# From attention to experts: the order of work at the border of two phases in a fused attention and mixture-of-experts kernel

## The chip, the cores and the metric

The kernel runs on one core of a Trainium2 chip. A core has a matrix engine (TensorE, PE in the profile, with its weight loads shown as PEld), a vector engine (VectorE, DVE), an engine for activations and copies (ScalarE, ACT), a general engine (GpSimd, POOL) and a queue engine that issues transfers (SyncE, SP). Each runs its own instructions in the order in which the program lists them and waits for the others through semaphores. The metric is the device time of one execution, in microseconds (us).

## The reference

Sliding-window attention with four sink tokens over 4 batches, 8 heads, 768 positions and 64 columns per head; its output, 3072 tokens of 512 columns, goes through a two-level mixture of experts.

```
scores = scale * q @ k.T, kept where key < 4 or 0 <= query - key < 128
a = exp(scores - max); a = a / (sum(a) + 1e-9); x = a @ v      # 3072 tokens x 512
g_idx = argmax(x @ w_group)             # 4 groups
e_idx = argmax(xg @ w_expert[g])        # 4 experts in each
h = relu(xg @ w1[g, e])                 # 512 -> 1024
out[token] = g_w * e_w * (h @ w2[g, e]) # 1024 -> 512
```

## The kernel before, in words

**Attention.** Tokens are taken in 24 tiles of 128 (NI = 24). One loop over i from 0 to NI+1 works on three tiles at once: tile i gets its scores, maxima (DVE) and exponentials (ACT); tile a = i-1 gets its probabilities transposed (`trans`, on PE, into the two-bank tile `tp`), copied out of PSUM (`evac`, ACT, into `pa`), masked by two selects for each half (POOL, `pu` and `pa`) and multiplied with the values (`values`, `sink_values`), the result copied to `xT` (`out_evac`, ACT); tile b = i-2 gets its routing logits (`logits`), is transposed back (`natural`, into the same `tp`), scaled by the reciprocal of its sums (`norm`, into `xt`) and written to the DRAM tile `xd` by SP. There is one `tp` only, so `sink_t` and `natural` can write it when both `evac` have read it. In the last two rounds, i = NI and NI+1, no new scores are left ("tail"): the score banks are given back and become a ring of four banks `ph` for the experts, and the experts' work begins between the attention's instructions.

**Routing.** Tiles form four batches of six. `route` is a generator of small DVE steps for a batch (argmax, counts, positions, gate weights `cw`, a table `tab` of token numbers), with two steps on PE. Batch 1's end names the fullest expert (rank 0), and its first 256 tokens are gathered during attention (`xg`, indirect transfers by POOL). Batch 2's end gives rank 0's third tile, the late tile; batch 3's end gives rank 1's gather indices and the order of all other experts ("eid", "x2" to "x15"). `routing(k, kinds)` advances these generators by k steps; `rb` is the list of batches that are not finished. The gate weights are written into `xd` by SP (`put_gates`), in front of the gathers that read them.

**Experts.** Each weight chunk (128 x 1024 float32, 512 KB) is loaded by SP (`prefetch`, into `rw`), rounded to float32r by ACT (`whi`) and its rest is subtracted by DVE (`wlo`). During attention a chunk is rounded in two halves, a half per round (`wjob`, the second half waiting in `half`); in the tail it goes whole, and a finished chunk then also calls `prefetch`. Tokens are split the same way: `xpose` transposes a gathered tile on PE, ACT copies the rounded part to `un`, DVE the rest. A product is made of three: rounded by rounded, rounded by rest, rest by rounded. `layer1_wide` goes over eight column chunks of 128, each with 12 matmuls; `split_h` makes ReLU and its split on ACT and DVE, DVE's part one chunk later. `layer1_narrow` handles a tile of up to 128 tokens with the tokens stationary, in two halves u of 512 columns. `PARTS[0]` holds rank 0's first 256 tokens and its late tile. `early_work` is the generator for the first of these: two transposes, then eight chunks, and the late tile's transpose behind chunk number LATE, counted from 0.

**Order.** All engines take their instructions in the order written by the program. In the tail that order is written by hand in the loop below; afterwards `spend(us)` advances a planned clock `clk` by the PE time of each piece and inserts routing steps and weight jobs as long as the planned DVE time `dve` is not more than DVELAG = 1.5 ahead. A routing step costs at least the pace of the moment.

Of the kernel before, what the change touches and what calls it, by code (L numbers as in the profile page):

```python
# [14 lines left out]
AF = mybir.ActivationFunctionType  # L15
ALU = mybir.AluOpType
# [5 lines left out]
P = 128  # L22
B, H, S, D = 4, 8, 768, 64
NT = S // P
NI = B * NT
# [3 lines left out]
NDC = DM // P  # L29
G, EG, F = 4, 4, 1024  # L30
NE = G * EG
# [21 lines left out]
RAW, RAWB = 5, 4  # L53
PACE = 1.8
RPACE = 0.8
DVELAG = 1.5
XLEAD = 9
PEGAP = 1.6
REND, TSTEP = 6, 16
UNITS = {7: 3, 9: 4, 10: 9, 13: 3, 16: 10, 17: 5, 19: 4, 20: 5, 21: 4, 22: 5, NI - 1: 6}  # L60
HC = 3
LATE = 5
RUN = 1
PELAG = 2.0
DMALAG = 2.2
# [4 lines left out]
PARTS = [[dict(r=0, j0=0, T=EC * P, last=False), dict(r=0, j0=EC, T=CAPT[0] - EC * P, last=True)]]  # L70
# [64 lines left out]
def moe_attention(tc, kqT, vN, vS, nsw, wgx, w1, w2, out):  # L135
    nc = Pinned(tc)
    v = nc.vector
    with ExitStack() as top, ExitStack() as att:
# [34 lines left out]
        vts, svs, env, bat = {}, {}, {}, {}  # L173
# [618 lines left out]
        def evac(i, g):  # L792
            e = env[i]
            pa = wk.tile([P, 4, P], F32, name="pa", bufs=2)
            nc.scalar.copy(pa.rearrange("p h (f q) -> p f h q", f=2),
                           env["tp"][:, :, 4 * g * D:4 * (g + 1) * D].rearrange("p f (h q) -> p f h q", q=D))
            e["pT", g] = pT = [pa]
            if i % NT:
                for dst, sg in ((pu[g], -1), (pa, 1)):
                    nc.gpsimd.affine_select(out=dst[0:D], in_=pa[0:D], pattern=[[0, 8], [sg, D]], compare_op=ALU.is_ge,  # L800
                                            fill=0.0, base=(sg - 1) // 2, channel_multiplier=-sg)
                pT.append(pu[g])
# [51 lines left out]

        def norm(i):
            xt = wk.tile([P, DM], F32, name="xt", bufs=2)
            v.tensor_tensor(xt.rearrange("p (c j d) -> p j c d", c=NDC, j=2),
                            env["tp"][:, :, 0:NDC * D].rearrange("p j (c d) -> p j c d", c=NDC),
                            env[i]["rc"].rearrange("p (c j) -> p j c", j=2)[..., None].to_broadcast([P, 2, NDC, D]), ALU.mult)
            nc.sync.dma_start(xd[i * P:(i + 1) * P, 0:DM], xt)  # L860

        bounds = [sum(BATCHES[:k]) for k in range(len(BATCHES) + 1)]
# [19 lines left out]
                pick = {SNAP: 0, SNAPB: 1, len(BATCHES) - 1: 2}.get(k)  # L882
                rb.append([[(id(lt), x) for x in range(nb)], route(bounds[k], nb, lt, pick), None])

        def routing(k, kinds=(None, "pe", "rd")):
            while k > 0:
                if not rb or not have.issuperset(rb[0][0]):
                    return False
                kind = rb[0][2] if isinstance(rb[0][2], str) else None
                if kind not in kinds or (kind == "pe" and state["clk"] < state["at"]):  # L890
                    return False
                rb[0][2] = r = next(rb[0][1], "end")
                k -= r if isinstance(r, int) else 1
                if tail:
                    dve(0.6 if kind == "rd" else 0.25)
                state["at"] = max(state["clk"] + state["gap"], state["dve"] + 0.4)
                if rb[0][2] == "end":
                    rb.pop(0)
            return True
# [6 lines left out]
        def spend(us):  # L906
            state["credit"] += us
            state["clk"] += us
            state["route"] = min(state["route"] + us, 4.0)
            pace = RPACE if "x2" in ready else 0.1  # L910
            while state["route"] > pace and state["dve"] < state["clk"] + DVELAG and routing(1):
                state["route"] -= pace
            if state["credit"] >= PACE and (state["done"] < XLEAD or "x1" in ready) and state["dve"] < state["clk"] + DVELAG and wjob():
                state["credit"] = min(state["credit"] - PACE, 2 * PACE)
# [33 lines left out]
        def weights(*k):  # L948
            while k not in wt:
                if not wjob(True):  # L950
                    raise RuntimeError("weights out of order")
            return wt[k]

        def layer1_wide(q):
            T, o, r = q["T"], q["o"], q["r"]
            comb = T < 240
            lag = []
            if q["m"] < T:
                q["hq"] = yp.tile([P, NFC, 32], F32, name="hq", bufs=2)
            for f in range(NFC):  # L960
                ph = ps_h.tile([P, 512], F32, name="ph")
                fs = slice(f * P, (f + 1) * P)
                for c in range(NDC):
                    hi, lo = weights(1, r, c)
                    st, sp = c == 0, c == NDC - 1
                    if comb:
                        if sp:
                            nc.tensor.matmul(ph[:, 0:T], lo[:, fs], xx[:, c, o:o + T], start=False, stop=False)
                        nc.tensor.matmul(ph[:, 0:2 * T], hi[:, fs], xx[:, c, o:o + 2 * T], start=st, stop=sp)
                        if not sp:  # L970
                            nc.tensor.matmul(ph[:, 0:T], lo[:, fs], xx[:, c, o:o + T], start=False, stop=False)
                    else:
                        nc.tensor.matmul(ph[:, 0:T], hi[:, fs], xx[:, c, o:o + T], start=st, stop=False)
                        nc.tensor.matmul(ph[:, 0:T], hi[:, fs], xx[:, c, o + T:o + 2 * T], start=False, stop=False)
                        nc.tensor.matmul(ph[:, 0:T], lo[:, fs], xx[:, c, o:o + T], start=False, stop=sp)
                src = ph[:, 0:T]
                if comb:
                    src = yp.tile([P, 224], F32, name="hc", bufs=HC)[:, 0:T]
                    nc.scalar.copy(src, ph[:, T:2 * T])
                    v.tensor_tensor(src, ph[:, 0:T], src, ALU.add)  # L980
                lag.append(split_h(q, f, src))
                if len(lag) > 1:
                    drain(lag[0])
                    lag.pop(0)
                next(lag[-1]) if not comb else None
                us = T / 200 + (0.24 if comb else 0.18)
                pop_todo()
                state["freed"] += 4 if q["last"] and f == NFC - 1 else 0
                yield us
            drain(lag[0])  # L990
# [32 lines left out]
        def layer1_narrow(q):  # L1023
            T, o, r = q["T"], q["o"], q["r"]
            q["hs"] = h = yp.tile([P, F], F32, name="hs", bufs=1)
            for u in range(2):
                ph = ps_h.tile([P, 512], F32, name="ph")
                us = slice(u * 512, (u + 1) * 512)
                for c in range(NDC):
                    hi, lo = weights(1, r, c)  # L1030
                    xh, xl = xx[:, c, o:o + T], xx[:, c, o + T:o + 2 * T]
                    st, sp = c == 0, c == NDC - 1
                    nc.tensor.matmul(ph[0:T], xh, hi[:, us], start=st, stop=False)
                    nc.tensor.matmul(ph[0:T], xl, hi[:, us], start=False, stop=False)
                    nc.tensor.matmul(ph[0:T], xh, lo[:, us], start=False, stop=sp)
                    state["freed"] += u if q["last"] else 0
                    yield 0.7
                nc.scalar.copy(h[0:T, us], ph[0:T])

        def hidden_t(q, u):  # L1040
# [127 lines left out]
        for i in range(NI + 2):  # L1168
# [4 lines left out]
            if i == NI:  # L1173
                state.update(gap=0.0, dve=state["clk"])
                sps.close()
                put_gates(MAXB)
                while later:
                    gather(*later.pop(0))
                ps_h = fl.enter_context(tc.tile_pool(name="ps_h", bufs=4, space=PSUM, side="right", reuse_waits="tile"))
                tail.append(ps_h)  # L1180
                next(ew)
                next(ew)
                if half:
                    half.pop()()()
            if live:
                load_v(i)
            if i == 1:
# [4 lines left out]
            if mid:  # L1192
                trans(a)
                evac(a, 0)
                evac(a, 1)
            if live and i != 1:
                scores(i, 0)
            if later and not gates:
# [37 lines left out]
                norm_logits(b)  # L1236
            if late:
                late()
            if mid:
                values(a, 0)  # L1240
                values(a, 1)
                sink_values(a)
                out_evac(a)
            put_gates(2 if live else MAXB)
            routing(UNITS.get(i, REND) if live else TSTEP, (None, "rd"))
            if live and i % 2:
                sums(i)
            if i >= CHOOK and (i % 2 or i > NI - 4):
                prefetch(min(RAW, len(raws) + (1 if live else RAW)))
            if not live:  # L1250
                wjob()
                next(ew, None)
        att.close()
        state.update(gap=PEGAP)
        ps_t = fl.enter_context(tc.tile_pool(name="ps_t", bufs=2, space=PSUM, side="left", reuse_waits="tile"))
# [293 lines left out]
```

## Time and profile before

| what | us |
|---|---|
| median of three runs | 495.21 |
| lowest and highest run | 494.78, 497.12 |
| the profiled execution's own time | 498.14 |
| its span, first to last instruction | 496.4 |
| PE busy in it | 478.7 |
| DVE, ACT, POOL busy in it | 376.1, 327.9, 168.1 |

A profile line gives the start, the duration, the engine, the operation, the tile written and the tiles read with their shapes, and, in brackets, how long the engine had been idle before and who released it. Every operation has the same line number here, because a helper records them all; tiles are told apart by their names. In stretches of time, the busy times stand in the order PE, PEld, DVE, ACT, POOL.

### The profile page before, as it was taken

How to read it: one execution, taken by the hardware profiler on the slowest of the kernel's cores; microseconds unless marked ns; L12 is line 12 of the kernel's file. 1: busy time of each engine (PE TensorE's matmuls, PEld its weight loads, DVE VectorE, ACT ScalarE, POOL GpSimd, SP SyncE). 2: the span in 40 equal slices, each digit the busy share in tenths (PEclk: the TensorE clock that was granted, in tenths of full speed). 3: DMA queues.
4: the chain of work that ended last, by engine and by line, in shares of the span. 5: the costliest groups of instructions: out<-in, count | busy, mean ns of one | idle time of the engine just before them, and what ended most of it. 6: DMA issues, size and time to landing. Idle time of an engine off the chain costs nothing. (4 is left out here: it accounts for less than half of the span.)

```text
span 496.4 us, 14618 instructions
## 1 busy us (share of the span) xinstructions
PE 478.7 (96%) x5399; PEld 403.7 (81%) x5399; DVE 376.1 (76%) x1175; ACT 327.9 (66%) x861; POOL 168.1 (34%) x276
## 2 busy tenths in 40 slices
PE   7998999999999999999999999999999999999992
PEld 6787788887888888988989789669876979798782
DVE  7475897899989889997814875487588997889831
ACT  4887888889895335676615765377446786868731
POOL 3564454563563012512313123212232453230311
PEclk9999999999999999999999999999999999999997
DMA  7877776877986458863952338697859996996200
GB/s 201 258 221 218 234 224 219 258 234 251 300 285 204 151 162 301 274 230 109 388 230 81 108 111 302 212 353 260 311 182 366 411 325 227 383 305 207 98 22 29
DMA packets 59216, 114.71 MB, mean 231 GB/s; under 512 B 9486, under 2 KB 21774, under 8 KB 59136
## 3 DMA queue, kind: packets, MB, share of 16 engines
q1 hardware_dynamic: 54256, 100.14, 59.8%
q0 software_dynamic: 4352, 13.26, 7.8%
q8 instruction: 44, 0.72, 0.6%
q10 hardware_dynamic: 528, 0.29, 0.3%
q14 instruction: 36, 0.29, 0.2%
HBM read 100.89 MB, written 13.24 MB: 230 GB/s over the span
## 5 line engine op out<-in xcount | busy, mean ns | idle before, releaser
L105 DVE TENSOR_TENSOR wlo<-rw,whi 128x1024 fp32r<-128x1024 f32 x112 | 134.0, 1219 | 23.0 <-ACT whi L105 21.8
L105 PE MATMUL ph<-un,whi 128*128 128x256 f32 (+4 forms) x576 | 130.8, 315 | 0.0
L105 PE MATMUL po<-whi,un 128*128 128x512 f32 (+2 forms) x384 | 126.9, 396 | 0.0
L105 POOL DMA_INDIRECT out<-ot,sidx x33 | 52.9, 1603 | 213.5 <-DVE ot L105 69.8
L105 ACT CAST whi<-rw 128x1024 fp32r<-128x1024 f32 (+1 forms) x116 | 115.6, 1021 | 8.3 <-PE po L105 4.7
L105 PE MATMUL ph<-un,wlo 128*128 128x160 f32 (+4 forms) x416 | 100.4, 266 | 0.0
L105 PEld LDWEIGHTS ph<-un,whi 128*128 128x128 f32 x576 | 94.1, 189 | 1.4
L105 PEld LDWEIGHTS po<-whi,un 128*128 128x128 f32 (+1 forms) x384 | 70.8, 186 | 25.1 <-issue 6.7
L105 ACT ACTIVATE pt<-sm,st 128x136 f32<-128x136 f32 x192 | 76.0, 399 | 18.8 <-DVE st L105 18.7
L105 PE MATMUL po<-wlo,un 128*128 128x512 f32 (+3 forms) x200 | 77.8, 390 | 0.0
L105 PEld LDWEIGHTS ph<-un,wlo 128*128 128x128 f32 x416 | 77.1, 189 | 0.8
L105 POOL DMA_INDIRECT xg<-xd,gidx x33 | 37.3, 1130 | 35.5 <-DVE idz L105 25.0
L105 DVE CUSTOM_DVE_ANT_0 sm<-ps,msk 128x136 f32<-128x136 f32 x192 | 45.6, 295 | 4.2 <-PE ps L105 1.4
L105 DVE TENSOR_TENSOR hc<-ph,hc 128x160 f32<-128x160 f32 (+2 forms) x64 | 22.0, 347 | 28.0 <-ACT hc L105 26.5
L105 PEld LDWEIGHTS po<-wlo,un 128*128 128x128 f32 (+2 forms) x200 | 36.3, 182 | 7.5
L105 PE MATMUL ps<-kb,qb 64*64 64x208 f32 (+1 forms) x768 | 38.9, 339 | 2.0 <-DMA qb<-in_kqT 1.9
L105 ACT ACTIVATE ot<-po,cg 128x512 f32<-128x512 f32 (+3 forms) x25 | 17.0, 680 | 30.1 <-PE po L105 30.0
L105 ACT ACTIVATION_READ_ACCUMULATOR pt<-sm,st 128x1 f32 x192 | 36.3, 189 | 0.0
L105 ACT COPY hc<-ph 128x160 f32<-128x160 f32 (+2 forms) x64 | 19.9, 311 | 23.8 <-PE ph L105 19.1
L105 ACT ACTIVATE un<-ph 128x256 fp32r<-128x256 f32 x40 | 15.4, 385 | 28.7 <-PE ph L105 25.3
L105 PEld LDWEIGHTS ps<-kb,qb 64*64 64x64 f32 x768 | 27.1, 136 | 7.2 <-issue 2.8
L105 POOL TENSOR_SCALAR_AFFINE_SELECT pu<-pa 64x512 f32<-64x512 f32 x40 | 27.6, 691 | 14.1 <-ACT pa L105 13.9
(199 smaller groups left out, 746.3 us busy)
## 6 DMA issues: line engine op xcount, KB each, us to landing
rw<-in_w SPq DMA_DIRECT2D x128, 512.0 KB
vv<-in_vN SPq DMA_DIRECT2D x24, 512.0 KB
kb<-in_kqT SPq DMA_DIRECT2D x23, 288.0 KB
qb<-in_kqT SPq DMA_DIRECT2D x24, 256.0 KB
xd<-xt SPq DMA_DIRECT2D x24, 256.0 KB
svr<-in_vS SPq DMA_DIRECT2D x4, 192.0 KB
xg<-xd,gidx POOLq DMA_INDIRECT x33
out<-ot,sidx POOLq DMA_INDIRECT x33
```

Of the source, the lines that this page charges most:

```text
L105: r = f(*a, **k)
```

## The change

It has seven parts. (1) In round NI the transposes and copies of the last tile's probabilities come before the two token transposes of the experts instead of behind them. (2) The last half of a weight that is open in round NI-1 is rounded and split in that round and not at the start of the next. (3) In chunk 0 of rank 0's first layer, and in the first half of its late tile, the products with the rest of the tokens come last, behind all others. (4) The late tile is transposed behind chunk 6 and not 5. (5) In the tail `norm` uses eight activations on ScalarE, one for each head, in place of one multiplication on VectorE; this concerns tiles 22 and 23. (6) Routing in round NI+1 stops when one batch is left, and the paces of later steps change: 0.8 from "eid" on instead of from "x2" on, 3.0 from "x15" on. (7) At the end of both tail rounds the next chunk of layer 1 is listed ahead of the weight job.

```
+REST = 3.0
-LATE = 5
+LATE = 6
 def norm(i):
+    if tail:
+        for h in range(H):
+            nc.scalar.activation(xt[:, h * D:(h + 1) * D], env["tp"][:, h % 2, h // 2 * D:(h // 2 + 1) * D],
+                                 AF.Copy, scale=env[i]["rc"][:, h:h + 1])
+    else:
         v.tensor_tensor(xt..., env["tp"]..., env[i]["rc"]..., ALU.mult)
...
-def routing(k, kinds=(None, "pe", "rd")):
+def routing(k, kinds=(None, "pe", "rd"), till=0):
     while k > 0:
+        if len(rb) == till:
+            return False
...
-    pace = RPACE if "x2" in ready else 0.1
+    pace = REST if f"x{NE - 1}" in ready else RPACE if "eid" in ready else 0.1
...
 # layer1_wide, for each of the four row chunks c
+    elif q is PARTS[0][0] and f == 0:
+        nc.tensor.matmul(ph[:, 0:T], hi[:, fs], xx[:, c, o:o + T], start=st, stop=False)
+        nc.tensor.matmul(ph[:, 0:T], lo[:, fs], xx[:, c, o:o + T], start=False, stop=False)
+        for k in range(NDC if sp else 0):
+            nc.tensor.matmul(ph[:, 0:T], weights(1, r, k)[0][:, fs], xx[:, k, o + T:o + 2 * T],
+                             start=False, stop=k == NDC - 1)
...
 # layer1_narrow, late tile, first half
+    held_back = q is PARTS[0][1] and u == 0
     for c in range(NDC):
...
-        nc.tensor.matmul(ph[0:T], xl, hi[:, us], start=False, stop=False)
+        if not held_back:
+            nc.tensor.matmul(ph[0:T], xl, hi[:, us], start=False, stop=False)
...
+    for c in range(NDC if held_back else 0):
+        nc.tensor.matmul(ph[0:T], xx[:, c, o + T:o + 2 * T], weights(1, r, c)[0][:, us],
+                         start=False, stop=c == NDC - 1)
...
 # the loop, round NI
-    next(ew)
-    next(ew)
-    if half:
-        half.pop()()()
...
     trans(a)
     evac(a, 0)
     evac(a, 1)
+if i == NI:
+    next(ew)
+    next(ew)
+    if half:
+        half.pop()()()
...
 if late:
     late()
+if i == NI - 1 and half:
+    half.pop()()()
...
-routing(UNITS.get(i, REND) if live else TSTEP, (None, "rd"))
+routing(UNITS.get(i, REND) if live else TSTEP, (None, "rd"), int(i > NI))
...
 if not live:
+    next(ew, None)
     wjob()
-    next(ew, None)
```

More of the change, by code (lines that the diff above doesn't have):

```diff
@@ L856, in norm @@
             xt = wk.tile([P, DM], F32, name="xt", bufs=2)
-            v.tensor_tensor(xt.rearrange("p (c j d) -> p j c d", c=NDC, j=2),
-                            env["tp"][:, :, 0:NDC * D].rearrange("p j (c d) -> p j c d", c=NDC),
-                            env[i]["rc"].rearrange("p (c j) -> p j c", j=2)[..., None].to_broadcast([P, 2, NDC, D]), ALU.mult)
+            if tail:
[3 more added lines that the diff above has]
+            else:
+                v.tensor_tensor(xt.rearrange("p (c j d) -> p j c d", c=NDC, j=2),
+                                env["tp"][:, :, 0:NDC * D].rearrange("p j (c d) -> p j c d", c=NDC),
+                                env[i]["rc"].rearrange("p (c j) -> p j c", j=2)[..., None].to_broadcast([P, 2, NDC, D]),
+                                ALU.mult)
             nc.sync.dma_start(xd[i * P:(i + 1) * P, 0:DM], xt)
@@ L1031, in layer1_narrow @@
                     xh, xl = xx[:, c, o:o + T], xx[:, c, o + T:o + 2 * T]
-                    st, sp = c == 0, c == NDC - 1
+                    st, sp = c == 0, c == NDC - 1 and not held_back
                     nc.tensor.matmul(ph[0:T], xh, hi[:, us], start=st, stop=False)
-                    nc.tensor.matmul(ph[0:T], xl, hi[:, us], start=False, stop=False)
+                    if not held_back:
+                        nc.tensor.matmul(ph[0:T], xl, hi[:, us], start=False, stop=False)
                     nc.tensor.matmul(ph[0:T], xh, lo[:, us], start=False, stop=sp)
                     state["freed"] += u if q["last"] else 0
-                    yield 0.7
+                    yield 0.467 if held_back else 0.7
+                for c in range(NDC if held_back else 0):
+                    nc.tensor.matmul(ph[0:T], xx[:, c, o + T:o + 2 * T], weights(1, r, c)[0][:, us],
+                                     start=False, stop=c == NDC - 1)
+                    yield 0.233
                 nc.scalar.copy(h[0:T, us], ph[0:T])
```

## The prediction

> **What bounds the kernel now.** I read the page's shares first, then busy time by stretches, then the order of time around the change, then the queues. The shares name TensorE; the stretches (columns: length, then busy time and instructions of PE, weight loads, DVE, ACT, POOL; clock; DMA share; GB/s) say where it is not full.
>
> ```profile
> span 496.4 us, 14618 instructions
> PE 478.7 (96%) x5399; PEld 403.7 (81%) x5399; DVE 376.1 (76%) x1175; ACT 327.9 (66%) x861; POOL 168.1 (34%) x276
> ...
> 150.90:154.30 3.40, 2.29 (x42) 1.94 (x41) 3.26 (x13) 3.05 (x6) 0.59 (x2) 1.00 0.92 274
> 154.30:168.00 13.70, 13.66 (x180) 12.97 (x180) 12.38 (x34) 4.44 (x9) 3.95 (x5) 1.00 0.61 191
> 168.00:169.00 1.00, 0.10 (x2) 0.12 (x2) 1.00 (x4) 0.38 (x1) 0.00 (x0) 1.00 0.22 80
> 169.00:484.00 315.00, 315.00 (x1921) 262.68 (x1921) 235.97 (x518) 194.26 (x351) 85.19 (x61) 1.00 0.67 236
> ```
>
> From 169 us on PE is busy 315.00 of 315.00 us: the experts' phase is a block of fixed length at full clock (1.00), and it can only start sooner. All that the change can win lies between 150.9 and 169: PE is idle 3.40-2.29 = 1.11, then 0.04, then 0.90 us, together 2.05. Nothing in the change touches PE's work before 150.9. So the question is how much of two holes closes. In order of time, the first hole:
>
> ```profile
> 150.03 0.71 DVE L105 TENSOR_REDUCE lt<-lw 128x40 f32<-128x320 f32 x1
> 150.14 0.19 ACT L105 ACTIVATION_READ_ACCUMULATOR pt<-sm,st 128x1 f32 x1
> 150.89 1.06 PE L105 MATMUL ph<-ident,xg 128*128 128x128 f32 x8
> 151.15 0.59 ACT L105 COPY xT<-po 128x512 f32<-128x512 f32 x1 [0.82 <-PE po L105]
> 151.63 1.08 ACT L105 CAST un<-ph 128x512 fp32r<-128x512 f32 x2
> 151.88 0.71 PE L105 MATMUL tp<-ident,pt 64*128 64x64 f32 x16
> 152.37 0.63 DVE L105 TENSOR_TENSOR un<-ph,un 128x512 fp32r<-128x512 f32 x1
> 152.53 0.67 PE L105 MATMUL lg<-wsd,xT 128*64 128x40 f32 x16
> 152.59 0.64 ACT L105 CAST whi<-rw 128x512 fp32r<-128x512 f32 x1
> 153.10 1.10 ACT L105 COPY pa<-tp 128x512 f32<-128x512 f32 x2
> 153.63 1.21 DVE L105 TENSOR_TENSOR wlo<-rw,whi 128x1024 fp32r<-128x1024 f32 x1
> 154.34 0.26 PE L105 MATMUL tp<-ident,sp 64*96 64x64 f32 x2 [1.15 <-ACT pa L105]
> 154.78 0.51 PE L105 MATMUL ph<-un,whi 128*128 128x256 f32 x2
> 156.39 0.69 PE L105 MATMUL po<-pu,vv 128*64 128x64 f32 x16
> ```
>
> PE finishes the logits, then stands 1.15 us until ACT has copied the probabilities of tile 23 (pa) out of the bank that the next transposes overwrite. ACT is late because the two expert copies (un, 1.08) and the half weight (whi, 0.64) are ahead of pa in its queue. The second hole:
>
> ```profile
> 164.93 0.31 PEld L105 LDWEIGHTS ph<-un,whi 128*128 128x128 f32 x2
> 165.45 0.98 POOL L105 DMA_INDIRECT xg<-xd,gidx  x1 [8.04 <-DVE idz L105]
> 166.33 0.31 PEld L105 LDWEIGHTS ph<-un,whi 128*128 128x128 f32 x2
> 167.10 1.22 DVE L105 TENSOR_TENSOR wlo<-rw,whi 128x1024 fp32r<-128x1024 f32 x1
> 168.24 1.08 DVE L105 SCALAR_TENSOR_TENSOR un<-ph,un 128x256 fp32r<-128x256 f32 x3
> 168.91 0.63 PE L105 MATMUL ph<-ident,xg 128*128 128x128 f32 x4 [0.90 <-DMA xg<-xd,gidx]
> ```
>
> A chunk of layer 1 takes PE 166.33-164.93 = 1.40 us. After the sixth chunk PE wants the late tile; its gather, issued at 165.45, serves PE 3.46 us later, and DVE, whose low halves (un) sit behind a weight's (wlo), releases the bank no sooner.
>
> **Part by part.** *Probabilities first, weight half a tile sooner.* Same instructions, new order. PE runs transposes of pt from about 150.9 (the exponentials end at 150.33), then xg, logits, sinks: by the starts above 0.65+0.99+0.60+0.44 = 2.68, so it is at chunk 0 by 153.6. ACT: xT to 151.74, pa 1.10 to 152.8, un 1.08 to 153.9; the half weight, 0.64, moves into the gap before xT (0.82 idle there) and costs nothing. Chunk 0 could start at 153.9 against 154.78: 0.9 won. DVE pays: wlo (1.21) now comes before the routing steps, the sums and the two un, which take 152.37-150.74 = 1.6 and 153.63-152.37 = 1.3: wlo ends at 152.2, un at 155.1, where it ended at 153.6.
>
> *Low halves last in chunk 0 and in the late tile's first half.* As many matmuls and weight loads, only reordered; this hides most of what DVE pays. Eight of the chunk's twelve matmuls (0.94 of 1.40) run to 154.8, the last four wait for un at 155.1 and end near 155.6; the values' matmuls follow at 155.7 against 156.39. Without any collision the first hole gives back 0.7.
>
> POOL's selects over pa start at 152.4 instead of 153.78 and then lie beside DVE's small two-input steps:
>
> ```profile
> 153.78 1.57 POOL L105 TENSOR_SCALAR_AFFINE_SELECT pu<-pa 64x512 f32<-64x512 f32 x1 [2.81 <-ACT pa L105]
> 155.42 0.65 POOL L105 TENSOR_SCALAR_AFFINE_SELECT pa<-pa 64x512 f32<-64x512 f32 x1
> 155.44 0.69 DVE L105 TENSOR_TENSOR av<-av,val 128x42 f32<-128x42 f32 x1
> 174.70 0.20 DVE L105 TENSOR_TENSOR av<-av,val 128x42 f32<-128x42 f32 x1
> ```
>
> A select beside wlo took 1.57 instead of 0.65, and the step av beside a select 0.69 instead of 0.20. In the new order two such steps (runb, ge) stand between wlo and un; one waits nothing to 0.65, so DVE loses 0 to 1.3, and the 0.7 shrinks to between 0.7 and nothing. I take 0.4: two waits of half a select make 0.65, of which I let half reach PE. The Trainium skill, "SBUF — State Buffer", the section on its two separate sides, says that VectorE with two SBUF inputs and a GpSimd operation that reads SBUF exclude each other for the whole instruction; the rows agree, and taken at its word with both steps caught early the first hole would give nothing and the sum be 0.9.
>
> *Late tile after the seventh chunk.* PE reaches it 1.40 later in its order: 168.0-0.4+1.4 = 169.0. The gather: till keeps the last batch's first six steps out of DVE, and the scaling of xt leaves DVE (0.69 twice), while the wlo before it starts later, since ACT now does chunk 1's relu ahead of whi. I put the gather 0.4 earlier, at 165.05, served at 168.5. The 0.90 goes entirely. Of the bank, un comes free sooner: six steps and a wlo no longer precede it. The copy and split of the late tile are needed one chunk (1.40) after the transposes: un 0.59 fits.
>
> *Three weight loads move in SP's queue.* The half weight's completion in the tail issued prefetches; one tile sooner it does not, so three loads of 512 KB go out behind the gates' and xt's writes:
>
> ```profile
> 151.91 3.32 SPq L105 DMA_DIRECT2D rw<-in_w  x2
> 157.54 2.74 SPq L105 DMA_DIRECT2D xd<-cw  x6
> 160.38 1.34 SPq L105 DMA_DIRECT2D xd<-xt  x1
> ```
>
> That is after about 160.5, with a fourth behind them: 2.1 MB at the 274 GB/s of the first stretch is 7.7 us, to 168.2, around the gather. Their casts come after chunk 7 (170 us), so the weights themselves are in time. The gather may share the engines and land between 168.5 and 169.5; PE arrives at 169.0, so between 0 and 0.5 is lost; I take 0, since the gather served in 3.46 had traffic beside it too (0.61 share). The Trainium skill, "DMA: Bandwidth & Descriptors", queues and rings, has each engine alternate between its queues packet by packet, which would keep the gather from standing behind all four; no run here shows this yet.
>
> *Outputs scaled on ACT.* Eight activations of 64 columns replace one DVE instruction, for tiles 22 and 23:
>
> ```profile
> L105 ACT ACTIVATE ot<-po,cg 128x512 f32<-128x512 f32 x20 | 13.8, 690 | 28.2 <-PE po L105 28.2
> L105 ACT ACTIVATE ot<-po,cg 128x256 f32<-128x256 f32 x1 | 0.5, 474 | 1.8 <-PE po L105 1.8
> 159.16 0.59 ACT L105 COPY xT<-po 128x512 f32<-128x512 f32 x1 [2.13 <-PE po L105]
> 163.16 0.39 ACT L105 ACTIVATE un<-ph 128x256 fp32r<-128x256 f32 x1 [2.18 <-PE ph L105]
> ```
>
> The rows give 0.84 ns a column and 258 ns fixed: 312 ns each, 2.5 us for eight at most. ACT stands 2.13 and 2.18 us at just these places, so at most 0.4 leaks into xT or a relu, which PE does not need for another chunk: nothing. With the cover gone it would cost 2.5.
>
> *Planner.* Following its due times by hand, the gather for expert 1 is issued behind the sixth instead of the fourth step of layer 2's first tile (2 x 0.70 = 1.4 later in PE's order), the gates of the last batch four steps later (2.8), weights 6 to 8 sooner; the paces 0.8 and 3.0 only spread small DVE steps that nothing but the final branch awaits.
>
> ```profile
> 176.14 2.71 SPq L105 DMA_DIRECT2D xd<-cw  x6
> 184.59 0.94 POOL L105 DMA_INDIRECT xg<-xd,gidx  x1 [0.30 <-issue]
> 192.31 1.03 PE L105 MATMUL tp<-ident,xg 128*128 128x128 f32 x8
> ```
>
> The second gather lands at 184.59+3.46 = 188.1, and PE wants it at 192.31: of 4.3 us, 1.4 go, 2.9 stay. Cost nothing.
>
> **Sum.** 0.4+0.9 = 1.3 us: span 496.4 to 495.1. The profiled execution took 498.14, the runs' median is 495.21 (494.78 to 497.12), whose difference is not of this stage; I take 1.3 from the median: 493.9. The ends are 0 and 2.05.
>
> **Rivals.** (1) *DVE refills the first hole.* Both steps wait for selects, un ends after 156, chunk 0 ends where it did; the second hole still closes: 0.9, 494.3. For it: the 0.69 step; against: only two such steps. (2) *The late tile still waits.* The moved loads push the gather 0.5 to 1 us out, so the later chunk does not do what it says: about 0.5 won, 494.7. For it: DMA 0.92 busy at the loads' old place; against: 0.5 us of slack. (3) *Both holes close whole:* 2.05, 493.2; past the 2.48 us that are 0.5% (about what a measurement of this kernel can tell from no change) only if waits hidden in busy PE vanish too. (4) *Slower: expert 1's gather waits for the gates.* The gates' six writes, 2.8 later in order, go behind five weight loads in SP's queue; worked out, they issue at 176.14+2.8-1.3 = 177.6 and are through by 180.4, ahead of the gather. Each further microsecond eats the 2.9; the kernel is slower once the gates are over 2.9+1.3 = 4.2 us later than that, and by 0.5% from 6.7, 497.7. Against: before, nothing of SP's lies near the gates but the loads that follow them.
>
> **Numbers.** Forecast 0.45; (1) 0.20; (2) 0.13; (3) 0.13, of it 0.09 past 0.5%; (4) 0.09, of it 0.07 past 0.5%. Faster 0.09, within 0.84, slower 0.07. The range takes (1) to (3) and the runs' spread of 0.4: 494.78-2.05 = 492.7, and 495.5 where next to nothing is won.
>
> **What would show it.** In the trace after: the transposes of pt ahead of xg; no PE wait on pa; chunk 0 near 153.9 with its last four matmuls perhaps waiting for un; eight short ACT instructions ahead of xT; PE's wait for the gather gone or under 0.5; the full block starting near 167.7 and as long as before. I am wrong if a new wait of PE appears behind 169, above all at expert 1's transposes or a weight, or if the block's length changes by over 1 us.

## The result, and the profile after

The changed kernel took 500.0 us (median of 17 runs, 495.31 to 501.41) beside 496.94 us for the kernel before (17 runs, 494.06 to 499.19): a ratio of 1.0063, interval [1.0045, 1.0081]. The forecast was 493.9 with a range of 492.7 to 495.5. Medians, ratios and intervals in this document leave out slow runs, those over 1.5% above the fastest of the same kernel. The profiled execution of the changed kernel took 500.62 us, its span 498.8.

First the page's shares and the same stretches as before (same columns), after the change:

```profile
span 498.8 us, 14624 instructions
PE 479.2 (96%) x5399; PEld 403.9 (81%) x5399; DVE 374.1 (75%) x1173; ACT 330.9 (66%) x877; POOL 161.0 (32%) x276
...
150.90:154.30 3.40, 2.31 (x35) 1.92 (x34) 3.26 (x12) 1.20 (x3) 2.37 (x4) 1.00 0.36 133
154.30:168.00 13.70, 13.62 (x174) 13.00 (x174) 10.37 (x34) 8.19 (x26) 0.98 (x1) 1.00 0.57 183
168.00:169.00 1.00, 0.03 (x1) 0.00 (x0) 0.27 (x1) 0.38 (x1) 0.00 (x0) 1.00 1.09 427
169.00:484.00 315.00, 313.05 (x1891) 262.06 (x1892) 235.62 (x519) 193.55 (x350) 79.05 (x61) 0.99 0.67 237
```

The first hole is as large as before (2.31 busy of 3.40; it was 2.29). The second has grown: PE stands through 168 to 169 and for another 1.95 us behind it, at a DMA share of 1.09 where it was 0.22. And the clock of the last stretch is 0.99, not 1.00.

The attention part ahead of all this ends at a different moment in every execution (148.4 to 151.6 us in the fourteen traces), so I count from the end of the last exponential. Its row, the first values of tile 23 (`po<-pu`) and the first row of layer 2 of rank 0 (`po<-whi,un`), after:

```profile
148.77 0.20 ACT L106 ACTIVATION_READ_ACCUMULATOR pt<-sm,st 128x1 f32 x1
...
155.04 0.69 PE L106 MATMUL po<-pu,vv 128*64 128x64 f32 x16
...
180.47 0.40 PE L106 MATMUL po<-whi,un 128*128 128x512 f32 x1
...
488.92 0.28 PE L106 MATMUL po<-whi,un 128*128 128x256 f32 x1
```

and the last two of them before (the first two stand in the prediction):

```profile
178.27 0.40 PE L105 MATMUL po<-whi,un 128*128 128x512 f32 x1
...
486.75 0.28 PE L105 MATMUL po<-whi,un 128*128 128x256 f32 x1
```

Last exponential 148.97 after, 150.33 before. Values: 155.04-148.97 = 6.07 after, 156.39-150.33 = 6.06 before, so the first hole gives nothing. Layer 2: 31.50 after, 27.94 before, so 3.56 us are lost between the values and layer 2. From there to the last matmul: 308.45 after, 308.48 before. The whole loss lies between the values and layer 2, some 25 us of the span.

The waits of PE behind 148 us, by tile and releaser (us in total, times, longest):

```profile
PE ph L106 <- DMA xg<-xd,gidx: 2.9, 1, 2.9
PE ph L106 <- DVE un L106: 1.0, 1, 1.0
```

The wait for `pa` is gone, and one for `un` of about the same size (1.02; it was 1.15) stands in its place; the wait for the late tile's gather is 2.9 where it was 0.90. The gather, SP's queue around it, and one-microsecond stretches behind it:

```profile
160.44 2.14 SPq L106 DMA_DIRECT2D rw<-in_w  x4
163.86 0.35 SPq L106 DMA_DIRECT2D xd<-xt  x1
166.48 10.59 SPq L106 DMA_DIRECT2D rw<-in_w  x6
```
```profile
164.36 0.98 POOL L106 DMA_INDIRECT xg<-xd,gidx  x1 [10.95 <-DVE sidx L106]
...
170.95 0.63 PE L106 MATMUL ph<-ident,xg 128*128 128x128 f32 x4 [2.92 <-DMA xg<-xd,gidx]
```
```profile
171.00:172.00 1.00, 1.00 (x8) 1.00 (x9) 0.00 (x0) 0.38 (x1) 0.00 (x0) 0.82 0.99 397
172.00:173.00 1.00, 1.00 (x7) 1.00 (x6) 0.77 (x3) 0.20 (x1) 0.00 (x0) 0.50 1.04 406
...
174.00:175.00 1.00, 1.00 (x3) 0.79 (x3) 0.00 (x0) 0.97 (x2) 0.00 (x0) 0.50 1.05 408
175.00:176.00 1.00, 1.00 (x6) 0.75 (x4) 0.56 (x1) 1.00 (x2) 0.00 (x0) 0.98 0.58 217
```

The gather served PE 170.95-164.36 = 6.59 us after its issue (3.46 before), with four weight loads issued from 160.44 on ahead of it and six more from 166.48. Soon after PE resumed, the granted clock fell to 0.50, until about 175. The lost clock, 0.18+3x0.50+0.02 = 1.7 us (the three are 172 to 175), and 2.92-0.90 = 2.0 us of longer wait make 3.7 where 3.56 were found.

### The profile page after: what moved, and what is told of

Read it like the earlier page. It is cut to its first block, busy times and chain, and to the rows that moved or that the text cites. A ratio compares the mean times of both kernels' runs of the same rounds, so it can differ in the third digit from the quotient of the medians.

```text
span 498.8 us, 14624 instructions
## 1 busy us (share of the span) xinstructions
PE 479.2 (96%) x5399; PEld 403.9 (81%) x5399; DVE 374.1 (75%) x1173; ACT 330.9 (66%) x877; POOL 161.0 (32%) x276
## 5 line engine op out<-in xcount | busy, mean ns | idle before, releaser
L106 POOL DMA_INDIRECT out<-ot,sidx x33 | 48.2, 1461 | 218.4 <-DVE ot L106 59.6
L106 POOL DMA_INDIRECT xg<-xd,gidx x33 | 35.9, 1086 | 43.5 <-DVE idz L106 21.6
L106 PE MATMUL ps<-kb,qb 64*64 64x208 f32 (+1 forms) x768 | 37.8, 333 | 1.8 <-DMA qb<-in_kqT 1.8
L106 PE MATMUL po<-pa,vv 128*64 128x64 f32 x768 | 30.8, 223 | 1.1 <-issue 1.0
```

The costliest lines, as they stand in the source:

```text
L106: r = f(*a, **k)
```

## The experiments

Each was timed against the kernel before, on the same chip. There were three chips, on which the kernel before had medians of 496.52 (27 runs), 498.91 (26) and 497.99 (32). The theory (L): the three loads that the half weight no longer issues in round NI run beside the gather and hold it. Rival P: rank 1's chunks, let out sooner, hold it. Rival O: the new order of ACT and DVE work makes the gather late. To these belong K, that PE's clock falls behind a pause, and D, that DVE's work ahead of the low halves `un` bounds the first hole. The table gives, in us from the end of the last exponential, the first values of tile 23, the late tile's gather's issue and the first row of layer 2, then PE's wait for that gather.

| kernel | values | gather | layer 2 | wait | against before, interval |
|---|---|---|---|---|---|
| before | 6.06 | 15.12 | 27.94 | 0.90 | |
| after | 6.07 | 15.39 | 31.50 | 2.92 | 1.0063 [1.0045, 1.0081] |
| loads back | 5.88 | 15.20 | 26.99 | 0.16 | 0.9997 [0.9968, 1.0025] |
| loads only | 5.98 | 15.05 | 34.10 | 5.20 | 1.0115 [1.0088, 1.0142] |
| kept busy, 38 | 5.89 | 15.22 | 29.84 | none | 1.0070 [1.0044, 1.0097] |
| half back | 6.11 | 15.44 | 27.12 | none | 0.9998 [0.9977, 1.0018] |
| change again | 6.06 | 15.38 | 31.14 | 2.58 | 1.0002 [0.9967, 1.0037] |
| kept busy, 30 | 6.72 | 16.04 | 30.21 | none | 1.0026 [0.9992, 1.0060] |
| DVE freed | 5.00 | 14.32 | 25.93 | none | 0.9926 [0.9890, 0.9961] |
| gather sooner | 5.19 | 13.33 | 26.76 | 0.56 | 0.9939 [0.9905, 0.9973] |
| loads only, again | 5.52 | 14.59 | 33.86 | 5.06 | 1.0060 [1.0017, 1.0103] |
| loads only, kept busy | 6.06 | 15.13 | 32.51 | none | 1.0052 [1.0021, 1.0083] |
| late tile at five | 6.68 | 17.53 | 30.51 | 1.28 | 0.9994 [0.9964, 1.0025] |
| DVE freed, again | 5.38 | 14.69 | 26.22 | none | 0.9942 [0.9909, 0.9975] |

**The loads put back.** The change, with the loads issued in round NI as before.

```
 if i == NI:
     next(ew)
     next(ew)
     if half:
         half.pop()()()
+    prefetch(RAW + RAWB)
```

> The changed kernel, with the three weight loads (rank 0's last two chunks and rank 1's first) issued in round NI again, ahead of the gates' writes, as before the change; nothing else. Theory L (the moved loads are the traffic that holds the late tile's gather: 6.6 us from issue to use instead of 3.5): PE's wait for the gather falls from 2.9 to under 0.5 us, the granted clock stays 1.00 behind it, and the kernel is 3 to 5 us faster than the change, 0 to 1.5 us faster than the kernel before. Rival P (the traffic is the loads of rank 1's chunks that the change lets out from 166.5 us on, earlier in order): wait still over 2 us and the clock at 0.5, about 500 us. Rival O (the gather is slow because of the new order on DVE and POOL): the same as P.

Its queue of SP, and the gather's user:

```profile
149.14 3.51 SPq L106 DMA_DIRECT2D rw<-in_w  x4
...
161.85 0.35 SPq L106 DMA_DIRECT2D rw<-in_w  x1
163.89 0.33 SPq L106 DMA_DIRECT2D xd<-xt  x1
166.52 6.81 SPq L106 DMA_DIRECT2D rw<-in_w  x6
```
```profile
164.40 0.98 POOL L106 DMA_INDIRECT xg<-xd,gidx  x1 [10.35 <-DVE sidx L106]
...
168.22 0.63 PE L106 MATMUL ph<-ident,xg 128*128 128x128 f32 x4 [0.16 <-DMA xg<-xd,gidx]
```

The gather serves PE after 3.82 us, PE waits 0.16, and the clock stays at 1.00. Rank 1's six chunks go out at 166.52 all the same: P falls. The rest of the change is in place: O falls. Layer 2 starts 0.95 sooner than before, 0.2% of the time, which the interval does not tell from nothing. So the rest of the change gains nothing that these runs can tell; its parts 5 to 7 were not tested one by one.

**The loads alone.** The kernel before, with the half weight's prefetch in round NI held back and nothing else.

```
-if tail:                       # in the completion of a weight
+if tail and not state.get("hold"):
     prefetch(RAW + RAWB)
...
+state["hold"] = True
 half.pop()()()
+state["hold"] = False
```

> The kernel before, with those three loads issued only at the end of round NI, behind the gates' and xt's writes; nothing else of the change. Theory L: the gather, issued near 165.4, is used 6 to 7 us later while PE is ready at 168.0, so PE waits 3.5 to 4.5 us instead of 0.9, the clock drops to 0.5 for some 4 us behind it, and the kernel is 4 to 6 us slower than the kernel before. Rivals P and O: a wait of about 0.9 and no difference over 1 us.

```profile
159.70 2.23 SPq L105 DMA_DIRECT2D rw<-in_w  x4
162.03 0.37 SPq L105 DMA_DIRECT2D xd<-xt  x1
166.32 0.33 SPq L105 DMA_DIRECT2D rw<-in_w  x1
```
```profile
163.42 0.98 POOL L105 DMA_INDIRECT xg<-xd,gidx  x1 [7.98 <-DVE idz L105]
...
171.14 1.09 PE L105 MATMUL ph<-ident,xg 128*128 128x128 f32 x4 [5.20 <-DMA xg<-xd,gidx]
```

Moving three loads costs 1.15% by itself (0.60% in the repetition on the third chip, below). The gather takes 171.14-163.42 = 7.7 us; one load alone follows it, so the loads ahead of it are enough. The wait is 2.28 longer than in the change: without the later place of the late tile, PE is there 1.5 us sooner (17.57 behind the last exponential, 19.06 in the change), and the gather serves it 0.8 later.

**PE kept busy.** The change with 38 matmuls of zeros ahead of the late tile's transposes, into the bank that these overwrite; later 30, beside the change once more on another chip.

```
 # xpose
+if early and q["j0"] == EC:
+    warm(38, tx.rearrange("p a b -> p (a b)")[:, 0:192])
```

> The changed kernel, with 38 idle matmuls (bf16, 192 columns, about 3.1 us together) on PE ahead of the late tile's transposes, written into the bank that the transposes overwrite. Theory K (the pause itself lowers the granted clock, and that costs about 2 us on top of the wait): the gather is used as late as before, within 0.5 us, but the clock stays 1.00 through 171 to 175 us, and the kernel is 1 to 2 us faster than the change. Rival (the clock drop has another cause, or costs nothing): no difference, or slower by up to 3 us.

> The changed kernel itself, as the ruler for the other three on the same chip. All theories: 2 to 4 us slower than the kernel before, PE waits 2.5 to 3.5 us for the late tile's gather and the clock stands at 0.5 for some 4 us behind it.

> The changed kernel with 30 idle matmuls (about 2.6 us) ahead of the late tile's transposes, fewer than in the first try, so that they end before the gather lands. Theory K (the pause lowers the clock, and this costs 1.5 to 2 us on top of the wait): a wait of 0.3 to 0.8 us stays, the clock stays 1.00, and the kernel is 1 to 2 us faster than the changed kernel of the same call. Rival: within 0.5 us of it, the clock's drop costs nothing that the runs show.

In both, the clock stays at 1.00 behind the late tile and layer 2 starts 1.66 (38 against after) and 0.93 us (30 against the change again) sooner, the latter in an execution whose first hole had cost 0.66 more. In the median times nothing is gained: 1.0070 beside 1.0063, and 1.0026 beside 1.0002. On the second chip the 2 to 4 us of loss that were expected of the change do not show in its time: it is level with the kernel before, whose runs there reach from 493.74 to 501.08, although its trace has the wait (2.58) and the halved clock. As the kernel before also met the gather with no time to spare, some of its executions there may have waited longer; none of them is traced, so this is open.

**The half weight back in round NI.** The change without its second part.

```
-if i == NI - 1 and half:
-    half.pop()()()
```

> The changed kernel without its second part: the open weight half is rounded and split in round NI again, behind the two token transposes. That puts the three loads back too, and puts wlo behind the tokens' low halves on DVE. Theory L: as with the loads alone put back, no wait for the gather over 0.5 us, 3 to 5 us faster than the change. Theory D (the first hole gave nothing because wlo stood ahead of the tokens' low halves on DVE): chunk 0 no longer waits 1.0 us for un, but for wlo instead, since the same DVE work is only reordered; the values start 5.6 to 6.1 us after the last exponential as in both kernels (6.06, 6.07). If instead wlo's place alone was the cause, they start 5.1 or earlier.

```profile
155.38 0.38 PE L106 MATMUL ph<-un,wlo 128*128 128x256 f32 x1 [1.24 <-DVE wlo L106]
```

The loads return to round NI and the second hole closes; in the first, PE now waits 1.24 for the weight's low half in place of 1.02 for the tokens'. Whichever DVE makes last is what PE waits for. That speaks for D.

**DVE freed.** The loads put back by the line shown above, and two routing steps in round NI-1 instead of six, so that the other four do not run between `wlo` and `un`.

```
-UNITS = {..., 22: 5, NI - 1: 6}
+UNITS = {..., 22: 5, NI - 1: 2}
```

> The changed kernel with the loads put back (as in the first experiment), and two instead of six routing steps on DVE in round NI-1; the other four are done in round NI, behind the tokens' low halves. Theory D (DVE's work ahead of the tokens' low halves is what keeps the first hole open): no PE wait for un in chunk 0, the values start 5.0 to 5.4 us after the last exponential instead of 5.9 to 6.1; PE then meets the gather sooner, whose wait grows from 0.2 to 0.5 to 1.0 us, so the whole is 0 to 0.5 us faster than with the loads put back alone. Rival A (ACT's two token copies bound the first hole): values at 5.8 or later, no wait for un.

> The change with the three loads put back and two instead of six routing steps in round NI-1, once more on another chip. If its gain is the change's and not that chip's: 0.4 to 0.9% under the kernel before, values matmuls 5.0 us and layer 2 25.9 us behind the last exponential. If the 0.74% of the first time leaned on a disturbed kernel before: 0 to 0.4%.

```profile
152.69 0.39 PE L106 MATMUL ph<-un,whi 128*128 128x256 f32 x1 [0.16 <-ACT un L106]
...
154.29 0.69 PE L106 MATMUL po<-pu,vv 128*64 128x64 f32 x16
```

The wait for DVE's half of `un` is gone (0.16 for ACT's is left), and the values follow 5.00 us behind the last exponential, 1.06 sooner than before: D holds. The wait for the gather does not grow to the 0.5 to 1.0 that was expected, since the gather itself is issued 0.88 sooner than with the loads back. Layer 2 starts 2.01 sooner than before, and in the repetition 1.72. On two chips it is faster than the kernel before, by 0.74% and 0.58%, and on the one where the change ran beside it 0.8% faster by medians than the change (495.2 beside 499.13).

**The gather issued sooner.** The same, with the routing steps that make the gather's list taken earlier in round NI+1.

```
+if i > NI:
+    routing(1, ("pe",))
...
+if i > NI:                       # ahead of norm_logits
+    routing(TSTEP, (None, "rd"))
```

> As the kernel with DVE freed, and in round NI+1 the product that places batch 2's token numbers runs ahead of chunk 2, and its steps up to the gather ahead of the logits' scaling. Theory: the late tile's gather is issued 1 to 1.7 us sooner relative to the last exponential, PE does not wait for it, and the transition ends 25.9 to 26.4 us after the last exponential (first matmul of layer 2; 27.9 in the kernel before, 27.0 with the loads put back): 1.0 to 2.0 us faster than the kernel before. Rival: DVE becomes late elsewhere (a new wait for un or wlo in chunks 2 to 6), 27 us or more.

The gather is issued 1.0 us sooner but serves PE 5.5 us after that: PE waits 0.56, and nothing is gained. Layer 2 at 26.76 lies between what the theory (26.4 at most) and the rival (27 or more) had. Why the gather took longer is open: SP issued one load 1.4 us ahead of it and six from 3.8 us behind it, and the mean DMA share from its issue to its use is 0.74, hardly more than the 0.70 of DVE freed, where PE had it within 3.6 us.

**The clock once more, and the late tile's place.** On a third chip, the loads alone, the same with 58 matmuls of zeros, and the loads put back with `LATE = 5`.

> The kernel before with the three moved loads alone, once more, as the base for the next kernel on the same chip. Both theories: PE waits about 5 us for the late tile, layer 2 starts 6 us later than before counted from the last exponential, and the time is 1.0 to 1.3% over the kernel before. Theory K (the clock falls after the pause) expects a granted clock of about 0.5 in the five microseconds behind the wait.

> The same with 58 matmuls of zeros on PE in front of the late tile's transposes (5.0 us at 0.087 us each), their result overwritten, so that PE does not stand while the gather is under way. The gather is not helped. Theory K (about 3 us of the 6 are the clock): the granted clock stays at 1.00 behind the late tile, layer 2 starts 2.5 to 3.5 us sooner than in the kernel without the zeros, and the time is 0.5 to 0.7% under it. Rival (the clock in the records is a sampling of a pause and costs nothing): the start of layer 2 and the time as without the zeros, within 0.2%.

> The change with the three loads put back and the late tile behind the sixth chunk as before. If the later place of the late tile is what closes the second hole: PE meets the gather 1.4 us sooner and waits 1.2 to 1.7 us for it; layer 2 starts 1.0 to 1.5 us later than with the loads back and the late tile behind the seventh chunk, counted from the last exponential (26.99 there), near 28.2. If the gather itself comes sooner through the rest of the change: a wait under 0.9 as before or none. Time within 0.3% of the kernel before either way.

The clock by stretches, first with the loads alone, then with the zeros:

```profile
165.00:170.00 5.00, 1.21 (x11) 1.00 (x9) 2.50 (x6) 0.61 (x2) 0.00 (x0) 0.95 1.03 355
170.00:175.00 5.00, 3.73 (x18) 3.76 (x19) 1.08 (x3) 0.63 (x2) 0.00 (x0) 0.50 0.27 111
175.00:180.00 5.00, 5.00 (x38) 4.46 (x38) 2.84 (x14) 0.91 (x3) 0.00 (x0) 0.87 0.02 3
```
```profile
165.00:170.00 5.00, 4.26 (x44) 4.15 (x43) 3.65 (x10) 0.87 (x3) 0.94 (x1) 1.00 1.01 397
170.00:175.00 5.00, 5.00 (x57) 5.00 (x55) 0.74 (x3) 0.59 (x1) 0.00 (x0) 1.00 0.30 116
175.00:180.00 5.00, 5.00 (x41) 4.33 (x40) 3.68 (x19) 1.17 (x4) 0.00 (x0) 1.00 0.00 0
```

The zeros keep the clock at 1.00. Layer 2 starts 1.35 us sooner, not the 2.5 to 3.5 expected: PE waits 0.7 for DVE before the zeros can begin, and they end at 173.00, 23.17 behind the last exponential, where the other kernel's late tile began at 22.19, so they overstay by 1.0. The medians, 501.66 (8 runs) without and 500.84 (12) with the zeros, lie close and the ratios, 1.0060 and 1.0052, overlap. Nor does the gain last in the trace: behind the start of layer 2 the kernel with the zeros takes 309.73 to the last matmul and the other 308.43, so both end 342.2 to 342.3 us behind the last exponential. Of these 1.3 us, 0.77 are two waits of PE for DVE near 345 and 348 us; why they arise is open. The mean granted clock of the timed runs moves with the zeros: medians of 0.990 without and 0.9945 with them, 0.9905 for the change again and 0.994 with 30 zeros (12 runs each). So the fall of the clock that K claims is shown in the records of many runs; what it costs is seen in the traces up to layer 2, and in the time of the kernel it is not shown. The loads alone cost 0.60% here, below the 1.0 to 1.3 expected.

With the late tile at five, the wait for the gather is 1.28, within the 1.2 to 1.7 expected:

```profile
169.16 0.98 POOL L106 DMA_INDIRECT xg<-xd,gidx  x1 [13.20 <-DVE sidx L106]
...
172.74 0.63 PE L106 MATMUL ph<-ident,xg 128*128 128x128 f32 x4 [1.28 <-DMA xg<-xd,gidx]
```

PE is there 2.3 us after the gather's issue and not 3.7 as with the late tile at six: the later place is what closes the second hole. Layer 2, though, starts at 30.51 instead of near 28.2, because three DVE steps were caught beside selects, and the clock fell behind a pause of 1.81 us already:

```profile
153.31 0.62 DVE L106 TENSOR_TENSOR ktmp<-oh,col 128x16 f32<-128x16 f32 x1
...
154.59 0.68 DVE L106 TENSOR_TENSOR runb<-runb,rs 128x16 bf16<-128x16 bf16 x1
...
155.46 0.56 DVE L106 TENSOR_TENSOR ge<-pos,edge 128x48 f32<-128x48 f32 x1
```
```profile
157.66 0.73 PE L106 MATMUL ph<-un,whi 128*128 128x256 f32 x4 [1.81 <-DVE un L106]
...
160.00:161.00 1.00, 1.00 (x24) 1.00 (x23) 1.00 (x3) 0.58 (x3) 0.00 (x0) 0.50 0.20 21
161.00:162.00 1.00, 1.00 (x11) 0.88 (x8) 0.43 (x2) 0.00 (x0) 0.00 (x0) 0.50 0.24 32
```

## Why the prediction was wrong

**The step that failed** is "Three weight loads move in SP's queue". It saw where the loads would go (four from 160.5; measured 160.44) and that "the gather may share the engines", and then put "between 0 and 0.5 is lost; I take 0". The term was 2.0 us of longer wait, against the forecast's 0.9 us of saving: 2.9 off. (Of the distance between 493.9 and 500.0, 1.7 us is not the change: the base was the median of three runs, 495.21, and seventeen gave 496.94.) Counted from the last exponential, the forecast had the gather issued at 165.05-150.33 = 14.72, served 3.46 later, and PE there at 18.67, half a microsecond behind it. Measured were 15.39, 6.59 and 19.06. So 0.67 came from the issue, which was later than before and not sooner, 3.13 from the gather's time, and PE's own lateness gave 0.39 back: 0.5 of slack became 2.9 of wait. The argument for 0, that the gather of before had traffic beside it too, took the share 0.61 of a stretch of 13.7 us; while that gather was under way it was lower, 0.48 over 165 to 170 and 0.22 in 168 to 169, where the change has 1.09:

```profile
165.00:170.00 5.00, 4.10 (x36) 3.92 (x35) 4.08 (x13) 1.58 (x4) 0.98 (x1) 1.00 0.48 127
```

That row lay in the trace before. It gives no size, but it shows that this gather was no example of one beside full queues. Rival (2) named this mechanism and gave it at most 1 us.

The Trainium skill, "DMA: Bandwidth & Descriptors", "Queues, rings and completion order", has each engine alternate between queues packet by packet. I drew from it that the gather would not stand behind the loads. The runs do not bear out what I drew: with the four loads ahead, 6.25 to 7.72 us in the four traces in which PE waited for the gather; without them, 3.5 to 3.8 in six traces and 5.5 in the one with the gather sooner. What the engines did with each packet, the trace does not show.

**A term was missing:** the clock. The prediction had "a block of fixed length at full clock", which holds only as long as PE does not stand. Up to the start of layer 2, the wait of 2.9 us costs itself and 1.7 more. The Trainium skill, "TensorE: Matmul & The Clock Gate", Part 1, has the clock halved after an idle window of about 3.4 us and restored after as much activity, the windows running freely. The length at half clock agrees: 1.7 us of clock were lost behind each of three pauses, which is 3.4 us at 0.50. The length of the pause does not: 2.92, 2.58 and once 1.81 us, all shorter than such a window, were followed by it, while one of 1.75 (kept busy, 30) was not. With so few of them, where the limit lies is open.

**The first hole** came out as rival (1): 0 instead of 0.4. PE reached chunk 0 3.18 behind the last exponential (forecast 3.57), then waited for `un`, which DVE ended at 154.32, 5.35 behind it (forecast 4.77). Two steps had been caught beside POOL's selects and took 0.62 and 0.45 where they had taken 0.17 and 0.21 before. That is 0.69 together, close to the 0.65 that the forecast put; what it had wrong is that only half of it would reach PE. All of it did, since the next matmuls in PE's order read `un`:

```profile
151.48 0.62 DVE L106 TENSOR_TENSOR runb<-runb,rs 128x16 bf16<-128x16 bf16 x1
...
152.29 0.45 DVE L106 TENSOR_TENSOR ge<-pos,edge 128x48 f32<-128x48 f32 x1
...
154.38 0.73 PE L106 MATMUL ph<-un,whi 128*128 128x256 f32 x4 [1.02 <-DVE un L106]
```

The Trainium skill, "SBUF — State Buffer", "SBUF: two separate sides", has such a pair exclude each other. The steps' 0.62 and 0.45 agree with it.

**What held.** The block behind the transition has its fixed length (308.4 to 308.7 us from the start of layer 2 to the last matmul in thirteen of the fourteen traces; 309.7 in the one with 58 zeros). The late tile's later place closes the second hole once the loads are back (0.16). The eight scalings took 1.73 and 1.75 us, less than the 2.5 at most, and PE waits for none of them. Expert 1's gather, of rival (4), is issued at 186.90, behind the gates' six writes from 181.07, and its user starts at 194.48 with no wait.

```profile
155.58 1.73 ACT L106 ACTIVATE xt<-tp,rc 128x64 f32<-128x64 f32 x8
...
162.08 1.75 ACT L106 ACTIVATE xt<-tp,rc 128x64 f32<-128x64 f32 x8
```
```profile
181.07 2.74 SPq L106 DMA_DIRECT2D xd<-cw  x6
...
186.90 0.94 POOL L106 DMA_INDIRECT xg<-xd,gidx  x1 [21.56 <-DVE idz L106]
...
194.48 1.03 PE L106 MATMUL tp<-ident,xg 128*128 128x128 f32 x8
```

## What to carry to other kernels

When work is moved, look at what its completion triggers: here a half weight carried three loads with it, and these, not the work, made the wait. Check each moved transfer against the latency-bound transfer that flies beside it, with the DMA share of exactly those microseconds and not of a long stretch. A hole that is bounded by a second engine's queue closes only when that queue is shortened, which here took fewer routing steps and not a new order.

## What the hardware showed that was not expected

A 128-row gather was used 3.5 to 3.8 us after its issue in six traces, 5.5 in a seventh for a reason that is open, and 6.2 to 7.7 us with 2 MB of loads issued from some 4 us ahead of it on. Pauses of TensorE of 1.81 to 2.92 us were followed by about 3.4 us at a granted clock of 0.50, so up to the start of layer 2 such a wait cost some 1.7 us more than it shows; in the two pauses of over 5 us the clock fell already during the wait and stayed down for 4.3 and 5.0 us behind it. And the same order of DVE and PE instructions gave PE a wait for `un` of 0.41, 0.41, 1.02, 1.08, 1.75 or 1.81 us from one execution to the next, by how many DVE steps fell beside a select and how early (three in the last two).
